# Attention and gated feed-forward on one core: the states' product by row halves, weights unstacked, unread products in the early idle time of PE, and a new order

## The chip, the cores and the metric

One core of a Trainium2 chip runs the whole program. The time is the device time of one execution in microseconds (us), as the median of several runs; a profile of one execution comes with it.

## The reference

For each of 8 batches and 8 heads there are 512 tokens `x` and 32 states of 64 numbers. Tokens attend to the states and the states to the tokens; what each reads goes, as 4608 tokens of 512 numbers, through a gated feed-forward layer with 1536 inner columns:

```
scores  = scale * x @ state.T          xread = softmax(scores) @ state
scores2 = scale * state @ x.T          sread = softmax(scores2) @ x
x   = concat([xread, sread]) as (8 * 544, 512)
out = ((x @ w_a) * (x @ w_b)) @ w_out
```

All of it is float32.

## The kernel before

**What is computed where.** For the 512 tokens of a batch the kernel never forms `xread`: it multiplies the states of a batch by `w_a` and `w_b` first ("the states' product", 32 states of 4 batches = 128 rows at a time) and then multiplies the result by the softmax. The feed-forward's inner columns are cut into 12 tiles `ft` of 128, taken in six chunks `c` of two. For a batch and a tile, layer 1 runs 12 matmuls into two PSUM tiles `ab` (weights `p_h`, `p_l`, moving `at_h`, `at_l`); ACT copies one half to `a_sb`, DVE multiplies it by the other; the result is split into `g_h`, `g_l`; layer 2 runs 12 matmuls with `wo` into four `acc` tiles.

**Split numbers.** PE multiplies fp32r, a shortened float32, in one pass, so each number is kept as a high part `_h` and a low part `_l`, and a product is high*high + high*low + low*high.

**The states' product.** `states(j)` loads the states of four heads (`p_raw`, twice over both halves of the partitions) and splits them into `sd_h[j]`, `sd_l[j]`. `weights(c, hp)` converts the weights of a pair of heads into a tile `wq`, in which for each head the high part stands on one half of the 128 partitions and the low part on the other ("stacked"); the class `Conv` does it, with ACT casts of 64 partitions. `project` then multiplies for one head `hh` of the pair:

```
for k, s in enumerate((sd_h, sd_l)):
    nc.tensor.matmul(ps, lhsT=s[hp // 2][:, 2 * (hp % 2) + hh, bg], rhs=w[c, hp][:, hh],
                     start=(k == 0), stop=(k == 1))
```

so two full matmuls (128 rows, 128 columns, 512 moving) into one `ms` tile of PSUM, which ACT copies to `sw_st` and SP stores to `scr` in DRAM. There are 9 groups of 4 pairs (chunks 0 to 2 for the second four batches, chunks 3 to 5 for both fours), so 36 pairs. Batches 0 to 3 take chunks 0 to 2 by `direct`, a float32 product of 64 rows and 32 columns. `place` says where a raw weight is loaded (`raw`, 2 buffers, or tiles not yet or no longer in use).

**The start.** Batches 0 and 1 are "wide": `scores` on PE into `ms`, ACT copies it to `e2` (one buffer, `e` in the profile), SP stores `e2` to `kept` in DRAM, PE transposes it, DVE and ACT make the softmax in `s_p`, PE transposes back, ACT writes `at_h`, and PE subtracts that with `neg` (minus the identity, a `wo` tile in the profile, written by ACT's first ACTIVATE) for `at_l`. Each batch has two groups of heads `g`. The tokens `x` have one buffer, so the next batch's load waits for the scores.

**The order.** Every operation is recorded as a unit with an estimated occupancy (`cost`). `plan` orders the units of all engines by due times, which two tables, `SHIFTS` and `RELEASES`, move; the engines get their programs in this order, and every instruction has the line of the loop that replays it (L1362). So rows are told apart by tile names. An engine works strictly in its order: an instruction that waits holds all behind it.

Of the kernel before, what the change touches and what calls it, by code (L numbers as in the profile page):

```python
# [10 lines left out]
F32 = mybir.dt.float32  # L11
# [9 lines left out]
P = 128  # L21
# [18 lines left out]
FIRST, EARLY = 4, 3  # L40

# [138 lines left out]
def alone(u):  # L180
    u.occ, u.lat = 2 * u.occ - 365, u.lat + u.occ - 365


class Recorder:
# [31 lines left out]
    def cost(self, u, eng, method, out, ins, kw):  # L216
# [5 lines left out]
        if eng == "PE":  # L222
# [8 lines left out]
            if sh[0] < P:  # L231
                o *= sh[0] / P * (.5 if args_k(kw) == D else 1)
            if method == "matmul" and "is_transpose" not in kw and ins[-1].dtype == F32 and not u.turned:
                o, u.turned = o + 365, True
# [49 lines left out]
class Engine:  # L284
# [367 lines left out]
def attn_moe(ctx, tc, xt, xn, sd, wl, w_out, out):  # L652
# [210 lines left out]
    class Attention:  # L863
# [9 lines left out]
        def load(self):  # L873
            x = att.tile([P, XW], F32, name="x", bufs=1).rearrange("p (g h s) -> p g h s", g=NG, h=2)
            self.st, self.x = x[:, :, :, S:], x[:, :, :, :S]
            for g in range(NG):
                nc.sync.dma_start(out=x[:, g], in_=xt[self.b, g])
# [527 lines left out]
```

## Time and profile before

| | |
|---|---|
| median of 3 runs | 692.98 us (691.25 to 693.87) |
| profiled execution | 692.49 us |
| its span, first to last instruction | 690.3 us |
| busy: PE, DVE, ACT | 668.0, 475.0, 398.4 us |
| mean granted TensorE clock | 0.992 |

The profiled execution is 0.5 us under the median; 2.2 us of it lie around the span. Where PE is busy without gaps the time is its amount of work; only where it waits can the order of other engines' work matter.

### The profile page before, as it was taken

To read this page: it belongs to the slowest core of one execution; us is meant where nothing else is said; L and a number is where in the kernel's file an instruction comes from. 1 tells how busy PE (TensorE), PEld (TensorE's weight loads), DVE (VectorE), ACT (ScalarE), POOL (GpSimd) and SP (SyncE) were. 2 spreads that over 40 slices of the span, in tenths; PEclk is the share of its full clock that TensorE was granted. 3 is DMA by queue.
4 is the path that set the end of the run, shared out by engine and by line. 5 is a ranking of instruction groups with operands and counts; after the bars stand their busy time and mean duration, and the time that the engine had idled before them with its cause. 6 is when DMAs were issued, how large, how long until landed. Compare 5 with 4: busy or idle time off the path is not lost.

```text
span 690.3 us, 10474 instructions
## 1 busy us (share of the span) xinstructions
PE 668.0 (97%) x3774; PEld 527.8 (76%) x3774; DVE 475.0 (69%) x931; ACT 398.4 (58%) x741; POOL 0.7 (0%) x6
## 2 busy tenths in 40 slices
PE   3699999999999999999999999999999999999997
PEld 1377777778778888777878888887688788888996
DVE  2899998767775777689985433345985699733592
ACT  3687879658868657656594423433463566532361
POOL 0000000000000000000000000000000000000000
PEclk9799999999999999999999999999999999999999
DMA  8977487797989978999579521315546356400130
GB/s 281 309 232 268 167 283 241 239 318 256 370 311 365 409 264 286 340 339 359 224 233 332 175 77 44 109 40 183 178 143 207 123 162 228 148 12 1 62 123 30
DMA packets 65747, 146.17 MB, mean 212 GB/s; under 512 B 6304, under 2 KB 15008, under 8 KB 65696
## 3 DMA queue, kind: packets, MB, share of 16 engines
q1 hardware_dynamic: 65696, 145.52, 61.5%
q8 instruction: 29, 0.48, 0.3%
q14 instruction: 22, 0.18, 0.1%
HBM read 96.73 MB, written 48.76 MB: 211 GB/s over the span
## 4 chain that ended last, share of the span: by engine, by line
PE 88%; DMA 7%; ACT 2%; DVE 1%; SPq 1%; issue 0%; ACTq 0%
PE ab L1362 42%; PE acc L1362 38%; PE ms L1362 9%; DMA scr<-sw_st 2%; DMA raw<-wl 1%; DMA x<-xt 1%; DMA scr<-wo 1%; DMA kept<-e 1%; SPq L1362 1%; DMA p_raw<-scr 1%; ACT sw_st L1362 1%; ACT wq L1362 1%; DVE stg L1362 0%; ACT y L1362 0%; ACT a_sb L1362 0%
## 5 line engine op out<-in xcount | busy, mean ns | idle before, releaser
L1362 PE MATMUL acc<-wo,g_h 128*128 128x512 f32 x816 | 251.8, 392 | 0.0
L1362 PEld LDWEIGHTS acc<-wo,g_h 128*128 128x128 f32 x816 | 152.1, 188 | 37.4 <-issue 3.4
L1362 PE MATMUL acc<-wo,g_l 128*128 128x512 f32 x408 | 149.9, 391 | 0.0
L1362 PE MATMUL ab<-at_l,p_h 128*128 128x512 f32 x360 | 139.8, 391 | 0.0
L1362 PE MATMUL ab<-at_h,p_h 128*128 128x512 f32 x360 | 139.2, 393 | 0.2 <-ACT p_h L1362 0.2
L1362 PE MATMUL ab<-at_h,p_l 128*128 128x512 f32 x360 | 135.2, 390 | 0.0
L1362 ACT CAST g_h<-a_sb 128x512 fp32r<-128x512 f32 (+1 forms) x108 | 64.6, 599 | 99.7 <-PE acc L1362 65.9
L1362 DVE TENSOR_TENSOR a_sb<-ab,a_sb 128x512 f32<-128x512 f32 (+1 forms) x108 | 71.0, 657 | 64.9 <-PE ab L1362 53.8
L1362 DVE TENSOR_TENSOR g_l<-a_sb,g_h 128x512 fp32r<-128x512 f32 (+1 forms) x108 | 70.5, 656 | 58.4 <-PE acc L1362 35.9
L1362 ACT COPY a_sb<-ab 128x512 f32<-128x512 f32 (+1 forms) x108 | 60.7, 562 | 53.8 <-PE ab L1362 48.7
L1362 PEld LDWEIGHTS acc<-wo,g_l 128*128 128x128 f32 x408 | 76.6, 188 | 16.9 <-issue 0.8
L1362 PEld LDWEIGHTS ab<-at_h,p_h 128*128 128x128 f32 x360 | 67.6, 188 | 18.1 <-ACT a_sb L1362 1.5
L1362 PEld LDWEIGHTS ab<-at_l,p_h 128*128 128x128 f32 x360 | 67.7, 188 | 16.9 <-issue 2.5
L1362 PEld LDWEIGHTS ab<-at_h,p_l 128*128 128x128 f32 x360 | 67.6, 188 | 14.0
L1362 DVE TENSOR_SCALAR t<-t 128x512 int32<-128x512 int32 x132 | 54.2, 421 | 21.3 <-ACT t L1362 19.6
L1362 DVE TENSOR_TENSOR p_l<-p_raw,p_h 128x512 fp32r<-128x512 f32 x72 | 47.3, 685 | 29.4 <-ACT p_h L1362 18.8
L1362 ACT CAST p_h<-p_raw 128x512 fp32r<-128x512 f32 x72 | 41.6, 620 | 35.6 <-PE ab L1362 30.3
L1362 ACT CAST wq<-t 64x512 fp32r<-64x512 f32 (+1 forms) x64 | 39.1, 619 | 6.0 <-DVE t L1362 2.4
L1362 DVE TENSOR_TENSOR stg<-acc,stg 128x512 f32<-128x512 f32 x54 | 36.2, 685 | 8.6 <-PE acc L1362 8.4
L1362 ACT COPY sw_st<-ms 128x512 f32<-128x512 f32 x58 | 33.0, 588 | 13.7 <-PE ms L1362 12.2
L1362 ACT ACTIVATE t<-raw 128x512 f32<-128x512 f32 x44 | 29.2, 672 | 4.4 <-DMA raw<-wl 3.5
L1362 DVE SCALAR_TENSOR_TENSOR t<-raw,t 128x512 f32<-128x512 uint32 x44 | 30.2, 686 | 0.5
(107 smaller groups left out, 652.5 us busy)
## 6 DMA issues: line engine op xcount, KB each, us to landing
raw<-wl SPq DMA_DIRECT2D x36, 512.0 KB, 5.7
p_raw<-scr SPq DMA_DIRECT2D x36, 512.0 KB, 4.7
scr<-sw_st SPq DMA_DIRECT2D x58, 256.0 KB, 5.2
part<-stg SPq DMA_DIRECT2D x26, 512.0 KB, 5.4
stg<-part SPq DMA_DIRECT2D x26, 512.0 KB, 6.5
x<-xt SPq DMA_DIRECT2D x16, 576.0 KB, 5.1
out<-stg SPq DMA_DIRECT2D x34, 256.0 KB, 4.5
x<-xn SPq DMA_DIRECT2D x16, 512.0 KB, 6.0
```

Source lines behind the costliest of these rows:

```text
L1362: getattr(obj, method)(*map(real, args), **{k: real(x) for k, x in kw.items()})
```

## The change

1. `states()` loads and splits the states of all heads once, an even head on partitions 0 to 63 and the odd head of the pair on 64 to 127: one `p_raw` instead of two, `sd_h` and `sd_l` of half the size in all.
2. `weights` leaves the pair as it is loaded: `wq[:, 0]` is the high part of both heads, `wq[:, 1]` the low part. One ACT cast of 128 partitions takes the place of three of 64.
3. `project` takes both heads at once: six matmuls with 64 rows, alternating between the lower and the upper half of the rows, into two `ms` tiles; three for each head (high*high, high*low, low*high), where low*low was computed too before.
4. 100 products of 256 columns with `neg` into an `ab` tile that nobody reads (`WARM`) are put on PE's queue.
5. The first load of `x` is cut in two; `raw` and `sw_st` get 3 buffers instead of 2; the places `sd_*` that later hold raw weights are two instead of four.
6. The planner's estimates move a little (365 to 400 ns for a tiled float32 unit, half time for 64 rows, `late`), and both tables are replaced, which changes the order on every engine.

```diff
+RAW, SWS, WQ = 3, 3, 4
+
+WARM, COLD = 100, 30
...
 def alone(u):
-    u.occ, u.lat = 2 * u.occ - 365, u.lat + u.occ - 365
+    u.occ, u.lat = 2 * u.occ - 400, u.lat + u.occ - 400
+
+
+def late(u, x):
+    u.occ, u.lat = u.occ + x, u.lat + x
...
-            if sh[0] < P:
+            if sh[0] < P or args_k(kw) == D:
                 o *= sh[0] / P * (.5 if args_k(kw) == D else 1)
...
 SHIFTS = {
-    0: 7451, 1: 1245, 2: 736, 3: -9782, 4: 112, 5: -19196, 6: -49076, 7: -29688, 8: -47176, 9: -7417, 10:
...
+    0: -18110, 1: -3185, 2: 414, 4: -258, 5: -660, 6: 599, 7: -1, 8: 14, 9: -1011, 10: -154, 11: 628, 12: -509,
...
+    if WARM:
+        ps = ps_ab.tile([P, 512], F32, name="ab")
+        for i in range(WARM):
+            u = nc.tensor.matmul(ps[:, :2 * P], lhsT=neg, rhs=neg.unsqueeze(1).broadcast_to([P, 2, P]), start=True, stop=True)
+            late(u, 95 if i < COLD else 0)
...
-    def states(j):
+    sds = []
+
+    def states():
         raw = mlp.tile([P, 4, B * NS], F32, name="p_raw")
-        nc.sync.dma_start(out=raw, in_=sd[:, 4 * j:4 * j + 4])
-        sd_h[j] = proj.tile([P, 4, 2, P], F32R, name=f"sd_h{j}", bufs=1)
-        sd_l[j] = proj.tile([P, 4, 2, P], F32R, name=f"sd_l{j}", bufs=1)
+        for hh in range(2):
+            rows = slice(hh * D, (hh + 1) * D)
+            nc.sync.dma_start(out=raw[rows], in_=sd[rows, hh::2])
+        sds.extend(proj.tile([P, 4, 2, P], F32R, name=f"sd_{x}", bufs=1) for x in "hl")
...
         def parts():
-            t = w[key] = proj.tile([P, 2, 512], F32R, name="wq", bufs=4)
-            return ((HI, t[HI, 1]), (LO, t[HI, 0])), ((ALL, t[:, 0]), (t[LO, 1], t[HI, 0]))
+            t = w[key] = proj.tile([P, 2, 512], F32R, name="wq", bufs=WQ)
+            return ((ALL, t[:, 0]),), ((ALL, t[:, 1]),)
...
-    def project(c, hp, bg, hh, psp, tag):
...
+    def project(c, hp, bg, psp, tag):
+        name, bufs = SW[st["n"] % (1 if 5 in opened else len(SW))]
+        sw, st["n"] = proj.tile([P, 2, 512], F32, name=name, bufs=bufs), st["n"] + 1
+        ps = [psp.tile([P, 512], F32, name=tag) for _ in range(2)]
+        h = 2 * (hp % 2)
         with rec.together(sw):
...
+            for k, (s, x) in enumerate(((0, 0), (0, 1), (1, 0))):
+                for i, rows in enumerate((LO, HI)):
+                    nc.tensor.matmul(ps[i], lhsT=sds[s][rows, hp, bg], rhs=w[c, hp][rows, x],
+                                     start=(k == 0), stop=(k == 2))
+        for i in range(2):
+            nc.scalar.copy(out=sw[:, i], in_=ps[i])
...
-                nc.sync.dma_start(out=x[:, g], in_=xt[self.b, g])
+                if self.b == 0 and g == 0:
+                    for h in range(2):
+                        late(nc.sync.dma_start(out=x[:, g, h], in_=xt[self.b, g, :, h]), 740 if h == 0 else 0)
+                else:
+                    nc.sync.dma_start(out=x[:, g], in_=xt[self.b, g])
...
-        ring = [("raw", 2)] * 2
+        ring = [("raw", RAW)] * 2
...
-            ring += [(f"sd_{x}{j}", 1) for x in "hl" for j in range(2)]
+            ring += [(f"sd_{x}", 1) for x in "hl"]
```

The next two blocks are PE's first instructions, before and then of the change. `ms<-x` are the scores, `acc<-ident,e` the transposes of the copied scores, `acc<-ident,s_p` the transposes back, `ab<-wo_94` the unread products (`wo_94` is `neg`).

```order
L1362 MATMUL ms<-x 32x512 x4
L1362 MATMUL acc<-ident,e_117 128x128 x4
L1362 MATMUL acc<-ident,s_p 128x128 x4
L1362 MATMUL ms<-x 32x512 x4
L1362 MATMUL acc<-wo_150,wo_99 128x512
L1362 MATMUL acc<-ident,e_173 128x128 x4
```

Now of the change:

```order
L1412 MATMUL ab<-wo_94 128x256 x21
L1412 MATMUL ms<-x 32x512 x4
L1412 MATMUL ab<-wo_94 128x256 x5
L1412 MATMUL acc<-ident,e_141 128x128 x4
L1412 MATMUL ab<-wo_94 128x256 x15
L1412 MATMUL ms<-x 32x512 x4
L1412 MATMUL ab<-wo_94 128x256 x11
L1412 MATMUL acc<-ident,s_p 128x128 x4
L1412 MATMUL ab<-wo_94 128x256 x7
L1412 MATMUL acc<-ident,e_213 128x128 x4
L1412 MATMUL ab<-wo_94 128x256 x32
```

The scores of the second group now stand before the transposes back of the first, and the unread products stand in front of nearly every early step.

The next two blocks are ACT's first instructions after the table load, before and of the change. `CAST sd_h` splits the states, `ACTIVATE s_p` is the exponential of the softmax, `ACTIVATE t<-raw` begins the conversion of a weight, `COPY e` copies scores.

```order
L1362 ACTIVATE wo_99<-ident 128x128
L1362 COPY e_117<-ms 128x512
L1362 CAST sd_h_128<-p_raw 128x4x4x32 x2
L1362 ACTIVATE s_p<-s_p 128x512
L1362 CAST wo_150<-acc 128x512
L1362 ACTIVATE t_152<-raw 128x512
L1362 ACTIVATE t_163<-raw 128x512
L1362 CAST sd_h_166<-p_raw 128x4x4x32
L1362 COPY e_173<-ms 128x512
```

Now of the change:

```order
L1412 ACTIVATE wo_94<-ident 128x128
L1412 COPY e_141<-ms 128x512
L1412 ACTIVATE s_p<-s_p 128x512
L1412 CAST sd_h<-p_raw 128x4x4x32 x2
L1412 ACTIVATE t_205<-raw 128x512
L1412 COPY e_213<-ms 128x512
L1412 CAST wo_221<-acc 128x512
```

The exponential stands before the casts of the states, and the second copy of scores (`e_173`, now `e_213`) has the cast of `at_h`, one conversion step and one cast of states less ahead of it.

The last two blocks are PE at one place of the states' product, before and of the change.

```order
L1362 MATMUL ms<-wq,sd_h_166 128x512
L1362 MATMUL ms<-wq,sd_l_924 128x512
L1362 MATMUL ab<-at_l,p_h 128x512
L1362 MATMUL ab<-at_h,p_l 128x512
L1362 MATMUL ab<-at_h,p_h 128x512
```

Now of the change:

```order
L1412 MATMUL ab<-at_h,p_h 128x512
L1412 MATMUL ms<-wq,sd_h 128x512 x4
L1412 MATMUL ms<-wq,sd_l 128x512 x2
L1412 MATMUL ab<-at_l,p_h 128x512
L1412 MATMUL ab<-at_h,p_l 128x512
```

Six matmuls of a pair stand together between full matmuls of layers 1 and 2, in the 36 places; before, a head's two stood alone or beside another head's two.

## Rows read from the trace of the kernel before

**Rows 1.** The page's first part: busy time of each engine, its share of the span, and its instructions.
```profile
...
PE 668.0 (97%) x3774; PEld 527.8 (76%) x3774; DVE 475.0 (69%) x931; ACT 398.4 (58%) x741; POOL 0.7 (0%) x6
...
```

**Rows 2.** Busy time by stage. Each row is one stretch (us from the span's start), its length, then busy us (and instructions) of PE, PEld, DVE, ACT and POOL, the granted TensorE clock as a share of full speed, the DMA share and GB/s.
```profile
...
0.00:17.30 17.30, 6.72 (x25) 2.12 (x25) 3.90 (x9) 6.02 (x9) 0.70 (x6) 1.00 0.80 280
...
20.70:24.10 3.40, 2.80 (x16) 0.23 (x8) 3.40 (x7) 1.20 (x3) 0.00 (x0) 0.50 0.79 286
...
27.50:34.40 6.90, 5.78 (x31) 3.90 (x32) 5.32 (x10) 3.67 (x8) 0.00 (x0) 0.51 0.97 331
...
40.00:80.00 40.00, 40.00 (x280) 29.33 (x279) 39.79 (x81) 31.87 (x61) 0.00 (x0) 1.00 0.62 212
...
140.00:380.00 240.00, 239.31 (x1264) 189.59 (x1263) 178.82 (x345) 164.41 (x300) 0.00 (x0) 1.00 0.88 314
...
```

**Rows 3.** The timeline of the first 45 us, all engines: start us, duration us, engine, line, operation, out<-in, shape, count, and in brackets the idle time before it and what ended it. SPq rows are issues of DMAs.
```profile
...
2.02 0.31 ACT L1362 ACTIVATE wo<-ident 128x128 fp32r<-128x128 f32 x1
...
4.12 1.93 PE L1362 MATMUL ms<-x 64*32 64x512 f32 x8 [4.12 <-DMA x<-xt]
...
6.12 0.58 ACT L1362 COPY e<-ms 128x512 f32<-128x512 f32 x1 [3.79 <-PE ms L1362]
...
6.85 1.09 PE L1362 MATMUL acc<-ident,e 128*128 128x128 f32 x4 [0.80 <-ACT e L1362]
...
8.71 0.69 DVE L1362 TENSOR_TENSOR s_p<-acc,m 128x512 f32<-128x512 f32 x1
8.96 2.00 ACT L1362 CAST sd_h<-p_raw 128x512 fp32r<-128x512 f32 x2 [2.25 <-DMA p_raw<-sd]
...
10.75 0.63 ACT L1362 ACTIVATE s_p<-s_p 128x512 f32<-128x512 f32 x1
...
13.38 1.12 PE L1362 MATMUL acc<-ident,s_p 128*128 128x128 f32 x4 [5.44 <-DVE s_p L1362]
...
14.43 1.93 PE L1362 MATMUL ms<-x 64*32 64x512 f32 x8
...
16.42 0.80 SPq L1362 DMA_DIRECT2D x<-xt  x2
...
18.60 0.63 ACT L1362 COPY e<-ms 128x512 f32<-128x512 f32 x1
...
19.26 0.33 SPq L1362 DMA_DIRECT2D kept<-e  x1
...
25.22 0.58 ACT L1362 COPY e<-ms 128x512 f32<-128x512 f32 x1 [1.70 <-DMA kept<-e]
...
31.62 1.48 PE L1362 MATMUL ab<-wo,p_h 128*128 128x512 f32 x3
...
```

**Rows 4.** The timeline of PE around 163 us: the states' product as it is (a product reads `wq` and a tile of the states). Successive starts give the spacing.
```profile
...
163.24 0.39 PE L1362 MATMUL ms<-wq,sd_h 128*128 128x512 f32 x1
163.46 0.39 PE L1362 MATMUL ms<-wq,sd_l 128*128 128x512 f32 x1
163.69 0.39 PE L1362 MATMUL ms<-wq,sd_h 128*128 128x512 f32 x1
...
```

**Rows 5.** The timeline of PE around 121 us: one unit of `direct` (weights of 64 rows and 32 columns, float32) between full 128x128 fp32r matmuls.
```profile
...
121.19 0.39 PE L1362 MATMUL ab<-wo,p_l 128*128 128x512 f32 x1
121.51 1.09 PE L1362 MATMUL ms<-sw_st,wo 64*32 64x512 f32 x16
122.53 0.72 PE L1362 MATMUL ab<-wo,p_h 128*128 128x512 f32 x2
123.10 0.40 PE L1362 MATMUL ab<-wo,p_l 128*128 128x512 f32 x1
...
```

**Rows 6.** The timeline of PE around 545 us: one float32 transpose through the whole array, between fp32r matmuls.
```profile
...
545.46 0.33 PE L1362 MATMUL ms<-ident,y 128*128 128x128 f32 x1
545.55 0.71 PE L1362 MATMUL acc<-wo,g_h 128*128 128x512 f32 x2
546.09 0.40 PE L1362 MATMUL acc<-wo,g_l 128*128 128x512 f32 x1
...
```

**Rows 7.** PE's groups with shapes kept apart (count, busy us, mean ns of one): the two forms of the states' product, and the form that rows 5 show one unit of.
```profile
...
L1362 PE MATMUL ms<-wq,sd_h 128*128 128x512 f32 x72 | 29.0, 403 | 0.3 <-ACT sw_st L1362 0.3
L1362 PE MATMUL ms<-wq,sd_l 128*128 128x512 f32 x72 | 28.2, 391 | 0.0
...
L1362 PE MATMUL ms<-sw_st,wo 64*32 64x512 f32 x64 | 4.4, 601 | 0.0
...
```

**Rows 8.** The timeline of PE around 563 us: twelve full-array fp32r matmuls of 256 columns, and the row after them.
```profile
...
563.34 1.59 PE L1362 MATMUL ab<-x,wq 128*128 128x256 f32 x12
564.77 0.63 PE L1362 MATMUL acc<-wo,g_h 128*128 128x512 f32 x2
...
```

**Rows 9.** ACT's groups with shapes kept apart (count, busy us, mean ns of one).
```profile
...
L1362 ACT COPY sw_st<-ms 128x512 f32<-128x512 f32 x58 | 33.0, 588 | 13.7 <-PE ms L1362 12.2 <-DMA scr<-sw_st 1.0
L1362 ACT CAST wq<-t 64x512 fp32r<-64x512 f32 x48 | 29.4, 618 | 3.7 <-PE ms L1362 1.7 <-DVE t L1362 1.0
...
L1362 ACT CAST wq<-wq 64x512 fp32r<-64x512 f32 x24 | 14.7, 619 | 2.9 <-DVE wq L1362 2.6
...
L1362 ACT CAST sd_h<-p_raw 128x512 fp32r<-128x512 f32 x4 | 4.2, 1105 | 2.3 <-DMA p_raw<-sd 2.3
...
```

**Rows 10.** Waits of PE's weight loads between 40 and 686 us: us in total, times, longest.
```profile
...
PEld ms L1362 <- ACT sw_st L1362: 2.8, 10, 0.7
...
```

More of the change, by code (lines that the diff above doesn't have):

```diff
@@ L230, in cost @@
                 o = n / .6
-            if sh[0] < P:
+            if sh[0] < P or args_k(kw) == D:
                 o *= sh[0] / P * (.5 if args_k(kw) == D else 1)
             if method == "matmul" and "is_transpose" not in kw and ins[-1].dtype == F32 and not u.turned:
-                o, u.turned = o + 365, True
+                o, u.turned = o + 400, True
             lat = o + 172
@@ L766, in attn_moe @@
     LO, HI, ALL = slice(0, D), slice(D, P), slice(0, P)
-    sd_h, sd_l = [None] * 2, [None] * 2
-    def states(j):
+    sds = []
+    def states():
         raw = mlp.tile([P, 4, B * NS], F32, name="p_raw")
-        nc.sync.dma_start(out=raw, in_=sd[:, 4 * j:4 * j + 4])
-        sd_h[j] = proj.tile([P, 4, 2, P], F32R, name=f"sd_h{j}", bufs=1)
-        sd_l[j] = proj.tile([P, 4, 2, P], F32R, name=f"sd_l{j}", bufs=1)
+        for hh in range(2):
+            rows = slice(hh * D, (hh + 1) * D)
+            nc.sync.dma_start(out=raw[rows], in_=sd[rows, hh::2])
+        sds.extend(proj.tile([P, 4, 2, P], F32R, name=f"sd_{x}", bufs=1) for x in "hl")
         for bg in range(2):
-            h, l = (t[j][:, :, bg].rearrange("p h (n b) -> p h b n", b=4) for t in (sd_h, sd_l))
+            h, l = (t[:, :, bg].rearrange("p h (n b) -> p h b n", b=4) for t in sds)
             r = raw[:, :, bg * P:(bg + 1) * P].rearrange("p h (b n) -> p h b n", b=4)
@@ L804, in parts @@
             if i % 2 == 0:
-                name, bufs = ("wq", 4) if c < 2 else ("sw_st", 2)
+                name, bufs = ("wq", WQ) if c < 2 else ("sw_st", SWS)
                 fw[c, i // 2] = proj.tile([P, 2, 512], F32R, name=name, bufs=bufs)
@@ L820, in attn_moe @@
     st = {"n": 0}
-    SW = ("sw_st", 2), ("wo10", 1), ("sw_st", 2)
-    def project(c, hp, bg, hh, psp, tag):
-        if hh == 0:
-            name, bufs = SW[st["n"] % (1 if 5 in opened else len(SW))]
-            st[bg], st["n"] = proj.tile([P, 2, 512], F32, name=name, bufs=bufs), st["n"] + 1
-        sw = st[bg]
-        ps = psp.tile([P, 512], F32, name=tag)
-        with rec.together(sw):
-            for k, s in enumerate((sd_h, sd_l)):
-                nc.tensor.matmul(ps, lhsT=s[hp // 2][:, 2 * (hp % 2) + hh, bg], rhs=w[c, hp][:, hh],
-                                 start=(k == 0), stop=(k == 1))
-        nc.scalar.copy(out=sw[:, hh], in_=ps)
-        if hh:
-            h = 2 * (hp % 2)
-            nxt.extend(lambda i=i: nc.sync.dma_start(
-                out=scr[c][bg][hp // 2, :, place_of(hp // 2, h + i)].rearrange("b n x -> n b x"),
-                in_=sw[:, i]) for i in range(2))
+    SW = ("sw_st", SWS), ("wo10", 1), ("sw_st", SWS)
+    def project(c, hp, bg, psp, tag):
[3 more added lines that the diff above has]
+        h = 2 * (hp % 2)
+        with rec.together(sw):
+            for k, (s, x) in enumerate(((0, 0), (0, 1), (1, 0))):
[4 more added lines that the diff above has]
+            nc.scalar.copy(out=sw[:, i], in_=ps[i])
+            nxt.append(lambda i=i: nc.sync.dma_start(
+                out=scr[c][bg][hp // 2, :, place_of(hp // 2, h + i)].rearrange("b n x -> n b x"), in_=sw[:, i]))
     xst = const.tile([P, 4, B, NS], F32, name="xst")
@@ L892, in scores @@
                 alone(u)
+            if self.b == 0 and gs == (0,):
+                late(u, 600)
         def copied(self, g):
@@ L982, in reads @@
         def reads(self):
-            self.a2 = proj.tile([P, NG, 4, 4, NS], F32, name="raw", bufs=2)
+            self.a2 = proj.tile([P, NG, 4, 4, NS], F32, name="raw", bufs=RAW)
             nc.sync.dma_start(out=self.a2.rearrange("p g h a n -> p (g h a n)"),
@@ L1121, in parts @@
                 if j == 0:
-                    name, bufs = ("sw_st", 2) if ft % 3 == 2 else ("wq", 4)
+                    name, bufs = ("sw_st", SWS) if ft % 3 == 2 else ("wq", WQ)
                     self.pieces[ft] = [proj.tile([P, 4, 256], F32R, name=name, bufs=bufs) for _ in range(2)]
@@ L1274, in products @@
         for hp in range(4):
-            for hh in range(2):
-                project(c, hp, bg, hh, *where)
+            project(c, hp, bg, *where)
         flush()
@@ L1301, in stack_chunk @@
         if not stacked:
-            for j in range(2):
-                states(j)
+            states()
         stacked.add(c)
```

395 rows, old and new, of tables (RELEASES, SHIFTS) are left out of this document.

## The prediction

> **What bounds the kernel now.** I read the page's busy times first: PE is busy for 668.0 us of a span of 690.3, DVE for 475.0 and ACT for 398.4 [rows 1]. Then the table by stage, to see whether that share holds everywhere. It doesn't: from 40 to 80 us PE is busy for all 40.0 us, and from 140 to 380 for 239.31 of 240, but in the first 17.3 us it is busy for 6.72 [rows 2]. So there are two regimes. After about 32 us PE works without gaps, and an edit there is worth exactly the PE time it adds or removes, whatever it does for ACT or DVE. Before that PE waits for a chain over four engines, and what counts is when that chain lets the stream of layer 1 begin, which is at 31.62 [rows 3]. One more thing is to be seen in the first stretch. The granted clock is 0.50 from 20.7 to 24.1 and 0.51 from 27.5 to 34.4, that is the lower of its two levels (1.2 GHz), and full later [rows 2]. Before 17.3 the column says 1.00, but the durations speak against it: the scores at 4.12 take 1.93 us [rows 3] where a unit of the same shape takes 1.09 at full clock [rows 5]. I take the engine as slow there too.
>
> **The states' product.** Successive products start 0.22 and 0.23 us apart [rows 4], so one takes 0.225, with full matmuls close on either side. A pair of heads needs four of them, 0.90 us, and the 36 pairs (72 + 72 records [rows 7]) 32.4 us. The new unit has six matmuls of 64 rows. If the lower and the upper half work at the same time, it has three slots of 0.225, which is 0.675, and what it costs to go into this form and out of it. That cost the trace doesn't show for fp32r. The nearest rows are the units of `direct`, which also use both row halves. From 121.19 to 123.10 there are 1.91 us with three full matmuls in them (0.675), so the unit costs 1.235 [rows 5]. Its work is 0.85: two records for each product, each 0.601 long [rows 7], less the tail of 0.176 that a full matmul has as well (0.39 long [rows 4], of which 512 columns at 2.4 GHz are 0.213). So entering and leaving costs 0.385 in float32. Part of it isn't the tiling: behind a float32 transpose through the whole array, two full matmuls take from 545.55 to 546.09, 0.54 where 0.45 is normal [rows 6]. That leaves at most 0.29 for the tiling. The bounds are 0 (fp32r after fp32r, rows 4, nothing lost) and 0.385. The new unit shares the number format and the width of 128 columns with the rows that lose nothing, and only the row halves with the rows that lose 0.29, so I take a third of it, 0.10. The unit is then 0.775 and saves 0.125; 36 of them save **4.5 us**. At the bounds the same edit saves 36 x 0.225 = 8.1 or costs 36 x 0.16 = 5.8.
>
> **The start.** This is a chain, and I follow it with the durations of rows 3. `neg` is ready at 2.02 + 0.31 = 2.33. Then 21 unread products stand before the first scores. At full clock twelve matmuls of 256 columns take 1.43 us [rows 8], 0.119 each; at half clock 0.24, so 21 take 5.0 and the scores start at 7.3 rather than 4.12. Against that, PE has been busy by then, and if the clock is up the scores take 1.1 rather than 1.93, and the copy of the scores comes at 8.4 rather than 6.12: 2.3 us late. Two things win it back. The exponential ran at 10.75 although its input was done at 9.40 (8.71 + 0.69), behind the two casts of states from 8.96; it now stands before them, which is worth 1.35. And the transposes at 6.85 need about half of their 1.09. So the transposes back come at 13.38 + 2.3 - 1.35 - 0.5 = 13.8, as good as before.
>
> The gain is behind that. The second scores stood behind the transposes back, at 14.43 to 16.36, and the load of the next batch's `x` waited for them until 16.42. They now follow the first transposes (end about 9.7) and 15 unread products (1.8): 11.5 to 12.6, and the load goes 3.7 us sooner. The second copy of scores was at 18.60; with fewer ACT steps ahead it comes behind the exponential (to 11.8), two casts (2.0) and one conversion step (about 0.7), at 14.5, 4 us sooner. Its store to `kept` went out at 19.26 and held the only buffer `e` until the copy of 25.22, which waited for that DMA by name. All of this moves 4 us ahead.
>
> I don't believe all 4 arrive. DVE is busy for 39.79 of the 40 us behind the start [rows 2] and has the same conversions and softmax steps to do before the stream can begin, so I hand on half: the stream begins at 29.6, **2.0 us** earlier. If the unread products keep the clock up, the stretch from 27.5 to 34.4 is at full rate; its 5.78 busy us [rows 2] hold 2.9 us of loss, of which I take half, **1.5 us**, since PE also waits for data there. Bounds for the start: 0 (DVE or the unread products eat it), and 4 + 2.9 = 6.9. The unread products themselves, some 15 us, lie where PE idles: 10.6 of the first 17.3 us and more up to 28; where they are in the way, as before the first scores, I counted them. The cut of the first load and the third `raw` buffer serve this chain and get no price of their own.
>
> **What is hidden.** Unstacking takes two of three casts of 64 partitions out of each of 24 conversions: (48 + 24) casts of 0.62 [rows 9] become 24 of the same length, about 30 us of ACT; two of four splits of the states, 2.2 us, go too [rows 9]. That is under PE: from 140 to 380 ACT is busy for 164.41 us of 240 and PE for 239.31 [rows 2]. It can give back no more than the 0.7 us that PE idles there; I count nothing. The rest of the order I count at nothing as well, with 1 us either way, for the few gaps that PE has.
>
> **One new wait.** A unit now needs both `ms` tiles. The next unit waits for two copies of 0.588 [rows 9], 1.2 us, on PE's queue, with all of layers 1 and 2 behind it. At present PE's weight loads stand 2.8 us in ten such waits [rows 10]. In the new order at least seven full matmuls, 1.6 us, lie between two units, so the copies fit if ACT is free. I count nothing, and 36 x 0.3 = 11 us if ACT comes late every time.
>
> **The sum**, against the profiled execution's 692.5 (the median is 0.5 higher): 692.5 - 4.5 - 3.5 = **684.5 us**.
>
> **The rivals.**
> - *Nothing is lost at the edges of a unit.* For it: rows 4. Then the product saves 8.1, and the time is 692.5 - 8.1 - 3.5 = 680.9. Chance 0.20.
> - *The start gives nothing*, since DVE sets its pace or the unread products delay the first scores by more than I think. Then 692.5 - 4.5 = 688.0. Chance 0.13.
> - *Each unit empties the array twice.* A matmul's tail is 0.39 - 0.225 = 0.165 us, at entry and exit 0.33; the unit is 1.005, which costs 36 x 0.105 = 3.8, and the time is 692.8; with the whole 0.385 of float32, 694.8. The Trainium skill, TensorEngine Tiling (Array Packing), section Tiling Modes, says just this: a change of the tiling mode drains the engine. By that rule the time would be 692.8, and the trace agrees so far as float32 units lose time at both edges; how much of it is the number format no row tells. Chance 0.15.
> - *The halves don't work at the same time* (slower than before). Six matmuls of 0.225 in turn are 1.35 a unit, 16.2 us more in all, and the time is 705.2. The edit turns from gain to loss at a unit of 0.90, and eats the start's gain at 1.0. Against it: the sixteen records of rows 5 take 1.02 us up to the next matmul; with the two halves in turn they would take 1.70. That is float32, though, where fp32r brings a column on each half in a quarter of the time. Chance 0.07.
>
> **How the numbers follow.** My forecast has the remaining 0.45, with 682 to 688 as its own range. What a measurement of this kernel can tell from no change is about 0.5%, 3.5 us, so "faster" is below 689.0. Forecast, first and most of the second rival lie there, 0.76; the rest of the second and the third, 0.16, are no change; 0.08 is slower. For 8 in 10 I reach from 679.5 (no loss at the edges, and 1.4 us more from the start) to 692, which leaves out the fourth rival and the upper half of the third.
>
> **What would show it.** The spacing from the full matmul before a unit to the one behind it, less one spacing: 0.78 by me, 0.68 by the first rival, 1.0 by the third, 1.35 by the fourth. The first `ab` matmul at about 29.6 with the clock full, not 31.62 at half. The copy of batch 1's scores near 21, not 25.2. ACT's busy time near 366. I would be wrong if the first scores come later than 8 and DVE's work follows them, or if PE's waits for `ms` go above 3 us.

## The result and the profile after

The changed kernel takes 698.12 us (median of 5 runs, 695.92 to 699.07) against 692.98 for the kernel before beside it; the ratio is 1.0078 with a 95% interval of 1.0049 to 1.0108. I had said 684.5. The profiled execution is the slowest of the five, 699.07 us; 1.8 us of it lie around its span of 697.3. So single places are read from its trace, and sums are compared with medians.

The page's busy line, which answers to [rows 1]. PE is busy 15.3 us longer (most of it the unread products), ACT 32.9 us less:

```profile
PE 683.3 (98%) x3946; PEld 529.7 (76%) x3946; DVE 474.9 (68%) x929; ACT 365.5 (52%) x691; POOL 0.7 (0%) x6
```

The table by stage with the stretches of [rows 2], the same columns:

```profile
0.00:17.30 17.30, 12.88 (x72) 10.15 (x73) 3.70 (x7) 4.47 (x6) 0.70 (x6) 0.90 0.91 251
20.70:24.10 3.40, 3.40 (x33) 2.88 (x31) 3.40 (x9) 2.17 (x4) 0.00 (x0) 1.00 0.77 304
27.50:34.40 6.90, 4.69 (x49) 3.07 (x46) 6.59 (x15) 4.84 (x12) 0.00 (x0) 1.00 0.96 329
40.00:80.00 40.00, 38.97 (x255) 27.23 (x254) 37.12 (x74) 27.57 (x52) 0.00 (x0) 1.00 0.68 223
140.00:380.00 240.00, 238.46 (x1303) 172.74 (x1302) 165.76 (x311) 134.79 (x254) 0.00 (x0) 1.00 0.85 296
```

The clock did come up: 1.00 from 20.7 to 24.1 and from 27.5 to 34.4, where it was 0.50 and 0.51. The durations agree: the scores at 23.56 take 1.06 us. (The column alone would not do: it reads 1.00 from 20.7 to 24.1 of x2_nowarm below too, where the scores at 21.29 take 1.93.) From 40 to 80 PE stands for 1.0 us where it stood for none; from 140 to 380 it works nearly without gaps as before, 238.46 us for 239.31. So the loss there must be more PE time, not waiting.

The timeline of PE at one unit of the states' product, which answers to [rows 4], and that of its weight loads there:

```profile
153.12 0.39 PE L1412 MATMUL ab<-at_l,p_h 128*128 128x512 f32 x1
153.35 0.39 PE L1412 MATMUL ab<-at_h,p_l 128*128 128x512 f32 x1
153.67 0.73 PE L1412 MATMUL ms<-wq,sd_h 64*128 64x512 f32 x4
154.24 0.39 PE L1412 MATMUL ms<-wq,sd_l 64*128 64x512 f32 x2
154.56 0.73 PE L1412 MATMUL acc<-wo,g_h 128*128 128x512 f32 x2
155.13 0.39 PE L1412 MATMUL acc<-wo,g_l 128*128 128x512 f32 x1
```

```profile
153.13 0.19 PEld L1412 LDWEIGHTS ab<-at_h,p_l 128*128 128x128 f32 x1
153.67 0.30 PEld L1412 LDWEIGHTS ms<-wq,sd_h 64*128 64x128 f32 x4 [0.35 <-issue]
...
154.56 0.30 PEld L1412 LDWEIGHTS acc<-wo,g_h 128*128 128x128 f32 x2 [0.37 <-issue]
```

The two halves do work at the same time: six matmuls take three slots (a slot is one normal spacing). But 153.35 to 153.67 is 0.32 where a normal spacing is 0.225; the first slot, the way out (154.24 to 154.56) and the two matmuls behind it (154.56 to 155.13, 0.57 for 0.45) are each about 0.1 too long as well. The load rows show what is lost: inside the stream the next weights are loaded as soon as a matmul starts, some 0.22 ahead of use; at both changes of form (from full matmuls to pairs of row halves, and back) the load stands idle (0.35, 0.37) and comes only at the switch. All 36 units have these two idle times, 0.35 to 0.37 us each. Over 36 units the median from the matmul before to the first normal one behind, less normal spacings, is 1.10 us. That is 0.42 for way in and out together, and 0.20 more than the 0.90 of four full matmuls. By the measure that I had named (to the matmul right behind the unit, less one spacing) it is 0.99, the third rival's 1.0; the 0.1 that is lost one matmul later lies outside that measure.

The timeline of the start, PE, then ACT, then SP's issues, against [rows 3]:

```profile
2.39 4.84 PE L1412 MATMUL ab<-wo 128*128 128x256 f32 x21 [2.39 <-ACT wo L1412]
7.16 1.06 PE L1412 MATMUL ms<-x 64*32 64x512 f32 x8
...
13.45 1.53 PE L1412 MATMUL ms<-x 64*32 64x512 f32 x8 [2.01 <-DMA x<-xt]
...
31.87 0.39 PE L1412 MATMUL ab<-wo,p_h 128*128 128x512 f32 x1
```

```profile
8.28 0.59 ACT L1412 COPY e<-ms 128x512 f32<-128x512 f32 x1 [5.95 <-PE ms L1412]
11.13 0.63 ACT L1412 ACTIVATE s_p<-s_p 128x512 f32<-128x512 f32 x1 [2.26 <-DVE s_p L1412]
15.64 2.09 ACT L1412 CAST sd_h<-p_raw 128x512 fp32r<-128x512 f32 x2 [3.88 <-DMA p_raw<-sd]
...
18.51 0.59 ACT L1412 COPY e<-ms 128x512 f32<-128x512 f32 x1 [0.33 <-DMA kept<-e]
...
24.69 0.59 ACT L1412 COPY e<-ms 128x512 f32<-128x512 f32 x1 [0.86 <-PE ms L1412]
```

```profile
0.74 0.86 SPq L1412 DMA_DIRECT2D x<-xt  x2
1.65 0.90 SPq L1412 DMA_DIRECT2D wo<-wl  x2
2.59 0.43 SPq L1412 DMA_DIRECT2D x<-xt  x1
3.07 2.21 SPq L1412 DMA_DIRECT2D p_raw<-sd  x2
...
8.90 0.34 SPq L1412 DMA_DIRECT2D kept<-e  x1
```

Scores, first copy and exponential come where I put them (7.16, 8.28, and 11.13 to 11.76). Then three DMAs end the waits: the second half of `x` (the tokens for the second group of heads), issued behind two loads of weights (second scores at 13.45 instead of 11.5 to 12.6); the states (casts at 15.64); and the store to `kept`, issued at 8.90, which frees `e` only at 18.5. The states' casts and the conversion step behind them hold ACT until 18.18, so the store adds only 0.33 here. The second copy is at 18.51, where it was at 18.60, the copy of batch 1's scores at 24.69, where I had put it near 21, and the first `ab` matmul at 31.87, where it was at 31.62. Two more executions of the same start, in x1_full and x3_edges below, have that matmul at 32.54 and 33.12. The early order gave nothing.

### The profile page after: what moved, and what is told of

Same layout as the page of the kernel before. It is cut to its first block, busy times and chain, and to the rows that moved or that the text cites. A ratio compares the mean times of both kernels' runs of the same rounds, so it can differ in the third digit from the quotient of the medians.

```text
span 697.3 us, 10747 instructions
## 1 busy us (share of the span) xinstructions
PE 683.3 (98%) x3946; PEld 529.7 (76%) x3946; DVE 474.9 (68%) x929; ACT 365.5 (52%) x691; POOL 0.7 (0%) x6
## 4 chain that ended last, share of the span: by engine, by line
PE 92%; DMA 4%; DVE 2%; ACT 1%; issue 0%; SPq 0%; DVEq 0%; ACTq 0%
PE ab L1412 44%; PE acc L1412 39%; PE ms L1412 9%; DMA kept<-e 3%; DMA x<-xn 1%; DVE t L1412 1%; DVE s_p L1412 0%; DVE m L1412 0%; ACT e L1412 0%; SPq L1412 0%; DVE wq L1412 0%; DVE wo L1412 0%; ACT L1412 0%; DVE g_l L1412 0%; ACT wo L1412 0%
## 5 line engine op out<-in xcount | busy, mean ns | idle before, releaser
L1412 PE MATMUL acc<-wo,g_h 128*128 128x512 f32 x816 | 242.1, 394 | 0.3 <-ACT g_h L1412 0.3
L1412 PE MATMUL acc<-wo,g_l 128*128 128x512 f32 x408 | 136.4, 392 | 0.0
L1412 PEld LDWEIGHTS acc<-wo,g_l 128*128 128x128 f32 x408 | 76.3, 188 | 17.8 <-issue 2.0
L1412 PEld LDWEIGHTS ab<-at_h,p_l 128*128 128x128 f32 x360 | 67.4, 188 | 17.8 <-issue 3.9
L1412 ACT COPY sw_st<-ms 128x512 f32<-128x512 f32 x58 | 31.5, 589 | 19.2 <-PE ms L1412 16.0
L1412 ACT ACTIVATE t<-raw 128x512 f32<-128x512 f32 x48 | 32.2, 673 | 11.9 <-DMA raw<-wl 4.0
L1412 DVE SCALAR_TENSOR_TENSOR t<-raw,t 128x512 f32<-128x512 uint32 x48 | 32.9, 686 | 0.6
L1412 ACT CAST wq<-t 128x512 fp32r<-128x512 f32 x40 | 24.8, 625 | 10.7 <-PE ab L1412 4.4
```

The costliest lines, as they stand in the source:

```text
L1412: getattr(obj, method)(*map(real, args), **{k: real(x) for k, x in kw.items()})
```

## The experiments

Each was timed in several rounds beside the kernel before, whose median there was 691.8 to 692.1; x3_edges ran once. The changed kernel wasn't timed again there, and the kernel before beside it had 692.98. So a difference from its 698.12 can be off by about 1 us, and I give it a second time "by the distances": each kernel less the kernel before beside it, +5.1 for the changed kernel.

The edits are shortened to the lines that say what changes. `u.swap` is what is replayed in the place of a unit's own calls.

**x1_full: four full matmuls.**

```diff
+        u.swap = [(base.tensor, "matmul", (ps[i],), dict(lhsT=sds[k][:, hp, bg], rhs=w[c, hp][:, i], start=(k == 0), stop=(k == 1)))
+                  for i in range(2) for k in range(2)]
```

> The changed kernel in its own order, but at each of the 36 places of the states' product four matmuls of 128 rows (each multiplies both halves of the states by both halves of the weights, so the numbers are not the reference's) stand where six of 64 rows stood. Theory A (going into and out of the row halves costs what the change lost): a place costs 0.91 us instead of 1.10, 36 x 0.19 = 6.9 us less, 691.2 us. Rival B (the new order and its waits cost it, the product's form does not): within 1.5 us of the changed kernel, 697 to 699.

690.75 us, ratio to before 0.9981 (0.9961 to 1.0001), 7.4 less than the changed kernel, by the distances 6.4: the first theory holds. PE's timeline at the same place, with spacings of 0.22 and 0.23 throughout:

```profile
153.22 0.39 PE L1414 MATMUL ab<-at_h,p_l 128*128 128x512 f32 x1
153.44 0.39 PE L1414 MATMUL ms<-wq,sd_h 128*128 128x512 f32 x1
153.67 0.39 PE L1414 MATMUL ms<-wq,sd_l 128*128 128x512 f32 x1
153.90 0.39 PE L1414 MATMUL ms<-wq,sd_h 128*128 128x512 f32 x1
...
154.35 0.62 PE L1414 MATMUL acc<-wo,g_h 128*128 128x512 f32 x2
```

**x3_edges: one more way out and in.**

```diff
+        full = (base.tensor, "matmul", (ps[0],), dict(lhsT=sds[0][:, hp, bg], rhs=w[c, hp][:, 0], start=False, stop=False))
+        u.swap = u.calls[:2] + [full] + u.calls[2:]
```

> The changed kernel with one full matmul of 128 rows put between the first and the second pair of row halves at each of the 36 places, so that each goes into and out of the row halves twice (the matmul adds a wrong term to the sum). Theory A (it is the edges that cost, 0.40 us for a way in and out): 36 x (0.227 + 0.40) = 22.6 us more than the changed kernel, near 720.7. Rival B (the six matmuls are slow by themselves, or the waits around them are): 36 x 0.227 = 8.2 us more, near 706.

719.51 us, 21.4 more than the changed kernel: 0.594 a unit, of which the full matmul itself is 0.225. So one more way out and in costs 0.37, by the distances (22.3 us more) 0.39. PE's timeline at the same place:

```profile
153.92 0.39 PE L1414 MATMUL ab<-at_h,p_l 128*128 128x512 f32 x1
...
155.77 0.50 PE L1414 MATMUL acc<-wo,g_h 128*128 128x512 f32 x1
```

From the matmul before the unit to the one behind it are 1.85 us, where the changed kernel has 1.21 (153.35 to 154.56); less the full matmul's 0.225 that leaves 0.41. Taking the edges away and doubling them give the same price, near 0.4; the first theory holds.

**x2_nowarm: no unread products.**

```diff
             late(u, 95 if i < COLD else 0)
+            u.swap = []
```

> The changed kernel without its 100 unread products, nothing else moved. Theory A (loads set the pace of the start, the unread products neither help nor harm by more than the clock): first scores near 4.2 us, first matmul of layer 1 between 31 and 33.5, the clock at half for some of the stretch before, time 698 to 700.5. Rival B (the 21 products ahead of the first scores hold the whole chain back by 3 us): first matmul of layer 1 near 29, time near 696.

695.16 us, ratio 1.0050 (1.0033 to 1.0066), 3.0 less than the changed kernel, by the distances 2.0; the interval overlaps that of the changed kernel (1.0049 to 1.0108). It is the second theory's time with the first theory's place of the first `ab` matmul, so neither. The first scores start at 3.64 and take 2.59 at half clock; the second scores still wait for `x`:

```profile
3.64 2.59 PE L1413 MATMUL ms<-x 64*32 64x512 f32 x8 [3.64 <-DMA x<-xt]
...
12.17 1.93 PE L1413 MATMUL ms<-x 64*32 64x512 f32 x8 [4.08 <-DMA x<-xt]
...
31.02 0.40 PE L1413 MATMUL ab<-wo,p_h 128*128 128x512 f32 x1
```

The store to `kept` goes out at 7.70 instead of 8.90 and the second copy comes at 17.47 instead of 18.51. So in this order the full clock that the unread products bring is worth no more than what they hold up, and probably less.

**x4_loads: the loads in order.** The second half of `x` and the states' two loads go ahead of the first two weights on SP.

```diff
+    sp = [i for i in order if rec.units[i].eng == "SP"]
+    front = sp[4:7]
+    order = [i for i in order if i not in front]
+    at = order.index(sp[2])
+    order[at:at] = front
```

> The changed kernel with three loads moved on SP's queue: the second half of the first tokens and both loads of the states go ahead of the first two loads of weights. Theory A (in the changed kernel these loads came late and ate the start's gain): second scores near 11.5 us instead of 13.45, casts of the states near 11.5 instead of 15.6, second copy of scores near 15.5 instead of 18.5, first matmul of layer 1 at 29.6 to 30.5 instead of 31.9, time 1 to 2 us less, near 696.5. Rival B (DVE sets the start's pace): first matmul of layer 1 at 31.5 or later, time within 0.7 us of 698.1.

694.06 us, ratio 1.0038 (1.0021 to 1.0055), 4.1 less than the changed kernel, by the distances 3.1, more than the 1 to 2 that I expected. The rival, a first `ab` matmul at 31.5 or later because of DVE, is out. The second scores are at 11.36 without a wait, the casts at 11.68, and the first `ab` matmul is at 29.96:

```profile
11.36 1.06 PE L1417 MATMUL ms<-x 64*32 64x512 f32 x8
...
16.03 0.58 ACT L1417 COPY e<-ms 128x512 f32<-128x512 f32 x1 [0.73 <-DMA kept<-e]
...
29.96 0.39 PE L1417 MATMUL ab<-wo,p_h 128*128 128x512 f32 x1
```

In these two traces 1.9 us of the gain lie at the first `ab` matmul, and 1.0 between 40 and 80 us, where PE is busy for all 40.00. Which of the two loads counts isn't separated.

**x5_both: both edits.**

> The changed kernel with both single edits at once: the second half of x and the states' two loads ahead of the first two weights on SP, and four full matmuls of 128 rows in the place of the six of 64 (on the same tiles, so the states' product computes other numbers; its time is that of the stacked product). Theory A, the two causes are independent and add: the load order gave 4.1 us, the full matmuls 7.4, so 698.1 - 4.1 - 7.4 = 686.6, between 685.5 and 688. Rival B, the load order's early gain is lost again in the product stage for another reason than the edges (ACT or DVE fall behind): no better than the full matmuls alone, 690 to 691.

686.91 us, ratio 0.9931 (0.9912 to 0.9950): 686.6 was the sum of the two, so the first theory holds. Edges and load order are two causes that add.

**x6_no21: without the first 21 unread products**, the loads as in x4_loads.

```diff
+            if i < 21:
...
+                u.swap = []
```

> The changed kernel with the three loads moved up, and without the 21 unread products that stand ahead of the first scores (the other 79 stay). Theory A, these 21 hold the chain: the first scores start near 4 instead of 7.16, at half clock, the first ab product near 28.5 to 29 instead of 29.96, and the time is 692.5 to 693.2 against 694.1 with the loads alone. Rival B, the full clock that the 21 bring from 7 us on is worth as much as the 3 us that they hold: first ab near 30, 694 to 695.

695.66 us, ratio 1.0050 (1.0033 to 1.0067), not better than x4_loads and a little over the rival's 694 to 695. The first copy comes 2.0 us sooner (6.29), but SP issues the store at 8.70 instead of 8.90 (what held SP wasn't followed up), and the second copy is at 16.25, released by it:

```profile
16.25 0.58 ACT L1420 COPY e<-ms 128x512 f32<-128x512 f32 x1 [0.76 <-DMA kept<-e]
```

**x8_border and x9_bwarm: the start's order in the kernel before**, without and with 59 unread products in gaps. The list moves a unit (engine and its place in the program) behind another.

```diff
+MOVES = [
+    ('PE 3', 'PE 1'), ('SP 11', 'PE 3'), ('SP 12', 'SP 11'), ('ACT 2', 'ACT 4'),
...
+    unread = {at(x): n for x, n in {'PE 0': 7, 'PE 2': 18, 'PE 6': 22, 'PE 8': 12}.items()}
```

> The kernel before, its product untouched, with the order of the change's start alone: the second scores behind the first transposes, the exponential ahead of the casts of the states, the second copy of scores right behind those casts, and its softmax ahead of the weights' conversions; no unread products. Theory A, the start can give about 2 us where the loads are in place: second copy near 13 instead of 18.6, the copy of batch 1's scores near 21 instead of 25.2, the first ab product at 29.5 to 30.2 instead of 31.6, time 689.5 to 690.7. Rival B, DVE or the loads of weights set the pace of the start: first ab later than 31, 691.5 to 692.5.

> The same as the run before it, with 59 unread products of 256 columns in gaps of PE: 7 ahead of the first scores, 18 ahead of the first transposes back, 22 and 12 further on. Theory A, in gaps they hold nothing and bring the full clock before 20 us: the stretch of half clock up to 34 us goes, 0.5 to 1.5 us less than without them, 688.5 to 689.7. Rival B, PE waits for data there, so the clock gives nothing: within 0.4 us of the run without them.

698.97 us, ratio 1.0096 (1.0083 to 1.0109), and 698.53, ratio 1.0095 (1.0080 to 1.0109): a miss, and the unread products make no difference that can be measured. They say little on the clock's worth: in x9_bwarm the second scores, at 7.94, still take 1.93 us, and from 20.7 to 24.1 the clock is 0.50. My list had put the loads of the next `x`, which wait for the second scores, ahead of the store to `kept` on SP. ACT and SP of x8_border:

```profile
20.41 0.58 ACT L1379 COPY e<-ms 128x512 f32<-128x512 f32 x1 [8.45 <-DMA kept<-e]
```

```profile
9.86 0.81 SPq L1379 DMA_DIRECT2D x<-xt  x2
12.27 9.08 SPq L1379 DMA_DIRECT2D kept<-e  x2
```

**x10_border2: the same with the store ahead again** (`('PE 3', 'SP 10')` for the first pair of the list).

> As x8_border (the kernel before with the order of the change's start), but the store of the first scores to kept stands ahead of the loads of the next batch's x on SP again, as in the kernel before, so that it is issued near 9 instead of 12.27. Theory A, x8_border lost its 7 us to that one store, which held the only buffer of the copied scores until 20.4: now the store lands near 16, as with the loads moved up in the changed kernel, the second copy comes near 16 instead of 20.41 (18.60 before), the first ab product near 30, and the time is 690 to 691.3. Rival B, the order itself is what costs: 696 or more. Rival C, the store's landing sets the pace, not the order: second copy later than 18, 691.5 to 692.5.

694.35 us, ratio 1.0029 (1.0015 to 1.0043). The store was worth 4.6 us, so the first theory has the cause of x8_border's loss; but its time was too good. The second scores are done by 10, and the copy stands until 16.65 for the store:

```profile
16.65 0.59 ACT L1379 COPY e<-ms 128x512 f32<-128x512 f32 x1 [4.55 <-DMA kept<-e]
```

The casts and conversions that I had put behind this copy wait with it, and the first `ab` matmul is at 32.78. No theory had this time.

**x11_full2: a whole version of both edits**, with the weights stacked again and the states of even and of odd heads each on 128 partitions. That needs two more tiles of 4 KB on each partition; `raw` and `sw_st` go back to 2 buffers for it.

```diff
-RAW, SWS, WQ = 3, 3, 4
+RAW, SWS, WQ = 2, 2, 4
...
+                u.then = [(base.scalar, "copy", (), dict(out=t[LO, 1], in_=f32(t[HI, 0]))),
+                          (base.scalar, "copy", (), dict(out=t[HI, 0], in_=f32(t2[LO])))]
```

> A whole version of the two edits: the changed kernel with the three loads moved up on SP, with 2 buffers each for raw and sw_st instead of 3 (so the planner's order shifts), the even and the odd heads' states each on all 128 partitions (two more tiles, loaded and split some 60 us before their first product), the weights stacked by three ACT casts of 64 partitions again, and four full matmuls for a pair. Theory A, the causes are edges and loads, and what ACT does more is hidden: ACT busy near 398 again, PE busy near 666, time 685.5 to 689, as with both single edits (686.91). Rival B, the smaller buffers or ACT's casts come late in the new order: PE's waits for wq or the raw loads show, 690 to 696.

755.86 us, ratio 1.0914 (1.0879 to 1.0949). Neither theory named this size, though the rival named the smaller buffers. The longest entry among the waits of PE's weight loads (total, times, longest) is for a buffer of `sw_st`, 0.7 us in the changed kernel:

```profile
PEld ms L1468 <- ACT sw_st L1468: 15.2, 17, 2.9
```

Two buffers in the place of three also change the planner's order, for which the tables weren't made. How much of the 69 us over x5_both each of these costs wasn't tested, so the run says nothing on the stacking.

**x12_late and x13_latefull: the states out of the start**, six and four matmuls a unit.

```diff
+    moves = [(i, 65e3) for i in sp[5:7]]
+    moves += [(i, 78e3) for i in order if name(i, "out") == "sd_h" and name(i, "in_") == "p_raw"]
+    moves += [(i, 80e3) for i in order if name(i, "out") == "sd_l" and name(i, "in0") == "p_raw"]
+    for i, t in moves + [(sp[4], 0)]:
...
```

> The changed kernel with x's second half right behind its first on SP, and with the states (which no product reads before some 140 us) out of the start altogether: their two loads of 256 KB, ACT's two casts and DVE's two subtractions stand some 50 us later, where DMA and DVE have room. Theory A, the start is paced by the DMA engines, whose busy share stood above 1.0 from 8 to 20 us at only 250 to 270 GB/s with the states' loads in that stretch (346 to 350 before), and by DVE behind it: kept lands sooner, the second copy comes near 15 (16.03 with the loads moved up), the first ab product at 28.5 to 29.4 instead of 29.96, time 692 to 693.2 against 694.06 with the loads moved up. Rival B, the chain of copies and of kept sets the pace whatever else is loaded: 693.7 to 694.6.

> The same with four full matmuls of 128 rows in the place of the six (on the same tiles, so the states' product computes other numbers; the time is that of the stacked product). Theory A, start and edges add: the run before this one less 7.2, so 685 to 686 (686.91 with the loads moved up). Rival B of that run: 686.5 to 687.5.

694.20 us, ratio 1.0037 (1.0026 to 1.0049), and 687.89, ratio 0.9939 (0.9922 to 0.9957). In the profiled execution of x12_late the store lands at 14.6 and the stream begins at 27.98, as the first theory said:

```profile
14.61 0.58 ACT L1424 COPY e<-ms 128x512 f32<-128x512 f32 x1 [0.73 <-DMA kept<-e]
...
27.98 0.39 PE L1424 MATMUL ab<-wo,p_h 128*128 128x512 f32 x1
```

But the median is that of x4_loads (694.06), as its rival said. That execution (692.81) is the fastest of its twelve, and two executions of the same start, of x4_loads and x5_both, began the stream 1.2 us apart. On the other hand x13_latefull's profiled execution, slower than its median at 688.45, begins at 27.89 too. Whether the 2 us are lost later or weren't there in most of the other runs stays open. x13_latefull is over both of its theories; its 6.3 us less than x12_late are a third price of the edges, 0.40 a unit (6.3 / 36 and the fourth slot).

## Why the prediction was wrong

**The product: the size of one term.** The unit's three slots, 0.675, were right. The edges were mis-sized: I took 0.10 between the bounds 0 and 0.385, and they are 0.42, by x3_edges about 0.4, above even the upper bound. So 36 units cost about 7 us where I had a gain of 4.5. The reasoning that failed is that the fp32r unit is "nearest" to the rows that lose nothing, since it shares their number format and width, and that 0.10 of the float32 edge is the format's. What the new unit shares with [rows 5] is that the form changes, and that is what costs: without the change, in x1_full, the loss is gone, and with twice as many, in x3_edges, it doubles. At each change the weights of the other form aren't loaded under the running matmuls; whether the late load is the cause or comes with it, the traces don't tell. The third rival had this mechanism, and I gave it a chance of 0.15. The range, to 692, left out both of its times, 692.8 and 694.8; that it left out the upper half alone, as the prediction says, is wrong. The Trainium skill, TensorEngine Tiling (Array Packing), section Tiling Modes, says that a change of the mode drains the engine; the traces agree, at about 0.2 us for each change.

**The start: a step left out.** The hand chain was right to the first copy (8.4, measured 8.28) and the exponential. From there it took the second scores from PE's program alone. SP's new order, with the second half of `x` behind two weights and the states behind that, had no term, nor had the DMA engines, whose busy share is 0.95 to 1.09 in that stretch. The table of 8 to 16 us for before, the changed kernel and x4_loads (the last two columns are the DMA share and GB/s):

```profile
8.00:12.00 4.00, 0.00 (x0) 0.00 (x0) 1.95 (x3) 2.42 (x3) 0.00 (x0) 1.00 1.05 346
12.00:16.00 4.00, 2.62 (x12) 0.92 (x12) 1.22 (x4) 0.69 (x2) 0.00 (x0) 1.00 0.95 350
```

```profile
8.00:12.00 4.00, 3.42 (x28) 2.90 (x24) 1.59 (x3) 1.22 (x2) 0.00 (x0) 1.00 1.07 251
12.00:16.00 4.00, 2.55 (x13) 1.24 (x14) 1.60 (x4) 0.36 (x1) 0.00 (x0) 0.74 1.09 268
```

```profile
8.00:12.00 4.00, 3.99 (x36) 3.04 (x32) 1.58 (x3) 1.45 (x3) 0.00 (x0) 1.00 1.02 345
12.00:16.00 4.00, 3.26 (x26) 2.67 (x22) 3.29 (x7) 2.41 (x3) 0.00 (x0) 1.00 1.07 367
```

As busy as before, the engines moved 251 GB/s instead of 346: that is where the states, cut by heads into pieces, were loaded. With the states out of the start, x12_late moves 350 there at a share of 1.04. That the size of the pieces is the cause isn't shown: from 8 to 16 us, 1084 of 1443 packets are under 2 KB, but before 637 of 1309 were too. And the store to `kept` bounds the second copy. Its landing, read from the copy that it releases, is 18.5 in the changed kernel, 16.0 in x4_loads, 16.65 in x10_border2, 20.4 in x8_border, each time with the second copy right at it. ACT stands for it alone in the last two (4.55 and 8.45 us); in the first two (0.33 and 0.73) other late loads hold ACT until shortly before. I had the single buffer `e` in the text, but no time for its store. The trace of before has it: the store goes out at 9.02 and takes 8.8 us, so `e` is free at 17.8, and with a store no sooner and no faster the second copy couldn't come at my 14.5. The row of the issue (KB, then us from issue to landing):

```profile
kept<-e SPq DMA_DIRECT2D x1, 256.0 KB, 8.8
```

The second rival had the start's outcome, but not its reason: the unread products delayed the first scores no more than I had reckoned, and x4_loads won by the order of loads alone, with DVE's work as it was.

**The clock.** That the unread products bring it up was right; the 1.5 us for it were not. Between 27.5 and 34.4 PE is busy for less (4.69 us for 5.78) and waits for longer (2.2 us for 1.1).

**Together.** With no edges the changed kernel is at 690.75, 1.3 under before and hardly apart from it (0.9961 to 1.0001), which is all that the start, the unread products and the rest of the order give. My own bounds, 0 for the start and 5.8 for the edges, add up to 692.5 + 5.8 = 698.3. That this is so near the measured time is luck, since the edges cost more and the rest gave a little; but I had weighed the bad ends one at a time, though nothing tied one to the other's good end.

**What held.** ACT's busy time (365.5, I said 366) and its being hidden; PE's loads for `ms` wait 0.7 us in all for ACT's copies, so the new wait on two tiles costs next to nothing. Neither of the signs that I had named for being wrong, late first scores and waits for `ms` copies over 3 us, appeared:

```profile
PEld ms L1412 <- ACT sw_st L1412: 0.7, 2, 0.4
```

## What to carry to other kernels

Where a group of matmuls of another form is put between full ones, price its way in and out from the nearest group that changes the form at all, not from one that shares the number format, and count how often it happens. In a start that waits, write the DMA issues into the chain beside the engines: which load stands ahead of which, and which store must land before a single buffer is free. When a term has a bad bound, add the bad bounds up once before setting the range.

## What the runs showed of the hardware

A change between full 128-row matmuls and pairs of 64-row matmuls, both fp32r, costs about 0.2 us each way, in the timeline as weight loads that stand 0.35 and 0.37 us idle; the float32 unit of [rows 5] had 0.385 for both ways, by the prediction's working. The first store to `kept`, 256 KB, took 6.2 (x12_late) to 9.7 us (x2_nowarm) from issue to landing while the DMA share was near 1.0. Where the states were loaded in pieces the engines moved 251 GB/s, 346 before, at the same share; the cause isn't shown.
